# A gated Fourier-mixing block on one core: LayerNorm statistics of the first chunk shared between VectorE and ScalarE

## Chip, core and metric

The kernel runs on one core of one Trainium2 chip. The metric is the device time of one execution in microseconds (us). Engines are named as in the profile: PE is TensorE's matrix multiply, PEld its weight load, DVE is VectorE, ACT is ScalarE, SP is the engine whose queue issues most transfers.

## What is computed

The input `x` has 2048 rows (tokens) of 512 numbers. Each row is normalised, the normalised matrix is mixed by a Fourier transform along both axes (real part), and the result is multiplied by a gate that a two-layer network computes from the same normalised rows.

```python
xn = (x - mean(x)) / sqrt(var(x) + 1e-5)            # per row, 512 numbers
a, b = xn @ Wd_re.T, xn @ Wd_im.T                   # 512 x 512
s = Ws_re @ a - Ws_im @ b                           # 2048 x 2048
h = relu(xn @ w1 + b1) ** 2                         # 512 -> 1792
g = silu(h @ w2 + b2)                               # 1792 -> 512
out = x + s * g
```

## The kernel before

Every product is made in fp32r from two parts of each operand: a high part (ACT copies the fp32 source into fp32r, `split_hi`, line 134) and a low part (DVE subtracts the high part from the source, `split_lo`, line 137). A product is three matmuls: high by high, high by low, low by high (`PASSES`).

The sequence transform comes first, in eight chunks of 256 output columns each. Chunks 0 and 1 are made plainly (`products`, matmuls on line 370), chunks 2 to 7 by a seven-product scheme (`mm`, line 355). The hidden-dimension transform (line 739), the first layer (line 739) and the second layer (line 845) follow. The order in which instructions stand on each engine is the order of the code: the schedule is manual, each engine works through its own list strictly from the front, and an instruction that waits holds back all that stand behind it.

The change is in **chunk 0**, lines 458 to 518, where the normalised input is also made. Chunk 0 has eight steps, j = 0 to 7. Step j treats 256 rows of `x`, as two halves of 128 (h = 0 and 1; half 1 lies 1024 rows further on). For a half, the names are:

- `x` (code: `xr[j]`): the raw rows, 128x512, loaded by SP (`load_x`, line 199). Four buffers.
- `bn_stats` and `bn_aggr` (`ln_stats`, lines 205 and 206, DVE): mean and variance into `stats`.
- the root of the variance (`ln_root`, line 213, ACT), then `ln_rstd` (lines 219 to 223, DVE): a reciprocal and one step of refinement, four tiny instructions.
- `xn` (`ln_xn`, line 230, DVE): the normalised half.
- `xc` high and low (`xc_parts`, lines 134 and 137): the parts of `xn`, the stationary operand of PE.
- `u` (`raw`, line 266): the raw columns of the sequence matrix, 128x1024 for a step, three buffers; `g` high and low (`plain_parts`): its parts, the moving operand, two buffers in turn.

PE's work in a step is 24 matmuls of 128x512 into four banks: for h = 0 and then h = 1, three groups of four (in chunk 0 all four high by high, then all four high by low, then all four low by high). So the first group of a half needs the high parts of `xc` and `g`, the second the low part of `g`, the third the low part of `xc`.

In step 0 the loads of `x` and `u` are split by halves, and 16 matmuls on zeros (line 475; 8 in bf16, 8 in fp32r) keep PE at work until the first operands are there. SP issues the loads in the order x0 (two halves), u0 (two halves), x1, u1, x2, u2, x3; later ones follow inside the loop, each when its buffer is free. In the loop, step j on DVE is: `ln_rstd(j)`, `xn` of both halves, `g` low, `xc` low of half 0, statistics of both halves of step j + 1, `xc` low of half 1.

After chunk 0, `plain_out` (ACT, line 144) takes the four banks out, and the sums and splits of the seven-product scheme (`sums`, line 248) begin on DVE beside chunk 1.

Of the kernel before, what the change touches and what calls it, by code (L numbers as in the profile page):

```python
# [10 lines left out]
AF = mybir.ActivationFunctionType  # L11
# [3 lines left out]
S, D, F = 2048, 512, 1792  # L15
# [3 lines left out]
NC = S // CW  # L19
TC = 512  # L20
NTC = S // TC
WARM = 8, 8
PLAIN = 2

ASIDE = 4.2
# [103 lines left out]
def fnet_gated_kernel(ctx, tc, x, xt, ct, wd, w1, w2, b1, b2, out):  # L129
    nc = tc.nc  # L130
    ctx.enter_context(tc.manual_schedule(engines=None))

    def split_hi(hi, lo, src):
        nc.scalar.activation(hi, src, AF.Copy)  # L134

    def split_lo(hi, lo, src):
        nc.vector.tensor_tensor(lo, src, hi.bitcast(F32), op=ALU.subtract)  # L137
# [5 lines left out]
    def copy(to, src, scale=1.0):  # L143
        nc.scalar.activation(to, src, AF.Copy, scale=scale)
# [7 lines left out]
    eps = pool.tile([P, 1], F32, name="eps")  # L152
    stats = pool.tile([P, 2, 2, NJ], F32, name="stats")
# [10 lines left out]
    def bank(tag, name):  # L164

        return acc.tile([P, 512], F32, tag=tag, name=name)

    def buf(tag, shape, name, dtype=F32):
        return pool.tile(shape, dtype, tag=tag, bufs=3 if tag == "u" else 1, name=name)

    def operand_buf(tag, name, step, shape=(2, 7, 256)):

        first = START.get(tag, 0)
        skip = (step - first) % 4 * LANE
        size = shape[0] * shape[1] * shape[2]
        room = ROOM.get(tag, 0)
        flat = buf(tag, [P, size + (room or skip)], name, F32R)
        a, b, c = shape
        return flat[:, skip:skip + size].rearrange("p (a b c) -> p a b c", a=a, b=b, c=c)

    def bcast(src, n):
        return bass.AP(tensor=src.tensor, offset=src.offset, ap=[[0, P], [1, n]])

    def halves(ap):
        return ap.rearrange("p (a b) -> p a b", a=2)
# [5 lines left out]
    small = buf("e", [P, 3, 16], "small")  # L191

    xr, xn32 = {}, {}

    def load_x(j, hs=slice(0, 2)):

        if j not in xr:
            xr[j] = buf(f"pq{j // 2 % 2}{j % 2}", [P, 2, D], f"x{j}")
        nc.sync.dma_start(xr[j][:, hs], x.rearrange("(h j p) d -> j p h d", h=2, p=P)[j][:, hs])

    def ln_stats(j, hs=slice(0, 2)):
        t = xr[j]
        for h in range(hs.start, hs.stop):
            bn = small[:, j % 3, 6 * h:6 * h + 6]
            nc.vector.bn_stats(bn, t[:, h])
            nc.vector.bn_aggr(stats[:, :, h, j], bn)

    root = {}

    def ln_root(j, hs=slice(0, 2)):  # L210
        n = hs.stop - hs.start
        t = root[j] = small[:, j % 3, 12:16]
        nc.scalar.activation(t[:, 0:n], stats[:, 1, hs, j], AF.Sqrt, bias=eps)

    def ln_rstd(j, hs=slice(0, 2)):
        n = hs.stop - hs.start
        y, q = root[j][:, 0:n], root[j][:, 2:2 + n]
        var = rstd = stats[:, 1, hs, j]
        nc.vector.reciprocal(y, y)

        nc.vector.scalar_tensor_tensor(q, var, EPS, y, op0=ALU.add, op1=ALU.mult)
        nc.vector.scalar_tensor_tensor(q, q, -0.5, y, op0=ALU.mult, op1=ALU.mult)
        nc.vector.scalar_tensor_tensor(rstd, q, 1.5, y, op0=ALU.add, op1=ALU.mult)

    def ln_xn(j, h):
        if j % ND == 0 and h == 0:
            xn32[j, "tile"] = buf(f"wd{j // ND}", [P, ND, 2, D], f"xn32_{j}")
        if h == 0:
            xn32[j] = xn32[j // ND * ND, "tile"][:, j % ND]
        nc.vector.tensor_scalar(xn32[j][:, h], xr[j][:, h], stats[:, 0, h, j:j + 1], stats[:, 1, h, j:j + 1],  # L230
                                op0=ALU.subtract, op1=ALU.mult)

    def xc_parts(j, h):
        s = slice(2 * h, 2 * h + 2)
        return XC[j][:, s, HI, :], XC[j][:, s, LO, :], halves(xn32[j][:, h])
# [26 lines left out]
    def load_c(c, j, hs=slice(0, 2)):  # L262
        if (c, j) not in raw:
            raw[c, j] = buf("u", [P, 8, CW], f"u{c}_{j}")
        q = slice(2 * hs.start, 2 * hs.stop)
        nc.sync.dma_start(raw[c, j][:, q], ct[c, j, :, q])

    def plain_parts(c, j, hs=slice(0, 2)):
        if (c, j) not in part:
            part[c, j] = operand_buf("g" + "ab"[j % 2], f"g{c}_{j}", 0 if (c, j) == (PLAIN - 1, NJ - 1) else 3 if j in TURNED else 1, (2, 4, CW))  # L270
        g, r = part[c, j], raw[c, j]
        s = slice(2 * hs.start, 2 * hs.stop)
        return g[:, HI, s], g[:, LO, s], r[:, s]
# [87 lines left out]
    def products(c, j, h):  # L361

        for passes in [PASSES] if c else [[q] for q in PASSES]:
            for k in range(ND):
                one_product(c, j, h, k, passes)
# [8 lines left out]
    one, two = slice(0, 1), slice(1, 2)  # L374
# [91 lines left out]
    load_x(3)  # L466

    warm = bank("b30", "warm")
    idle = buf("wd1", [P, 768], "idle")
    for count, zeros in zip(WARM, (idle[:, 0:256].bitcast(mybir.dt.bfloat16), idle[:, 256:768])):  # L470
        nc.vector.memset(zeros, 0.0)
        if zeros.dtype == F32:
            zeros = zeros.bitcast(F32R)
        for _ in range(count):
            nc.tensor.matmul(warm, zeros[:, 0:P], zeros, start=True, stop=True)
    ln_stats(0)
    ln_root(0)
    split_hi(*plain_parts(0, 0, one))
    ln_rstd(0)
    for h, hs in enumerate((one, two)):  # L480
        ln_xn(0, h)
        split_hi(*xc_parts(0, h))
        if h == 0:
            split_hi(*plain_parts(0, 0, two))
    for hs in (one, two):
        split_lo(*plain_parts(0, 0, hs))
    split_lo(*xc_parts(0, 0))
    ln_stats(1)
    g = plain_parts(0, 1)
    split_hi(*g)  # L490
    ln_root(1)
    split_lo(*xc_parts(0, 1))
    for h in range(2):
        products(0, 0, h)
    load_c(0, 3)
# [1 line left out]
    for j in range(1, NJ):  # L497
        ln_rstd(j)
        for h in range(2):
            ln_xn(j, h)  # L500
            split_hi(*xc_parts(j, h))
        split_lo(*g)
        load_c(*order[j + 3])
        if j + 4 < NJ:
            load_x(j + 4)
        split_lo(*xc_parts(j, 0))
        if j + 1 < NJ:
            ln_stats(j + 1)
            ln_root(j + 1)
        split_lo(*xc_parts(j, 1))  # L510
        for h in range(2):
            products(0, j, h)
        g = plain_parts(*order[j + 1])
        split_hi(*g)
        if j == 2:
            nc.sync.dma_start(b1s, b1)
            nc.sync.dma_start(b2s, bcast(b2, D))
# [62 lines left out]
    for n, s in enumerate(steps):  # L580
        c, j = s
# [4 lines left out]
        for p in FIRST if j == 0 and c > PLAIN else ORDER:  # L586
# [5 lines left out]
            a, b = PRODUCTS[p]  # L592
# [161 lines left out]
    class YUnit(Unit):  # L754

        y = None
# [183 lines left out]
    for u in range(2, NC):  # L940
        n = 2 * u + 2
# [82 lines left out]
    for n in range(NTC * NP):  # L1024
        c, p = divmod(n, NP)
# [102 lines left out]
def _launch(arrays, out_shape):  # L1128
    import numpy as np
    import concourse.bacc as bacc  # L1130
    from concourse.bass_utils import run_bass_kernel_spmd

    nc = bacc.Bacc("TRN2", target_bir_lowering=False, num_devices=1, dynamic_dma_scratch_size=1024)
    feed, args = {}, []
    for name, v in arrays.items():
        v = np.ascontiguousarray(v)
        feed[f"in_{name}"] = v
        args.append(nc.dram_tensor(f"in_{name}", v.shape, mybir.dt.from_np(v.dtype), kind="ExternalInput").ap())
    args.append(nc.dram_tensor("out_0", out_shape, F32, kind="ExternalOutput").ap())
    with tile.TileContext(nc, schedule_with_timeline_sim=True) as tc:  # L1140
        fnet_gated_kernel(tc, *args)
    r = run_bass_kernel_spmd(nc, [feed], core_ids=[0])
    return r.results[0]["out_0"]
# [25 lines left out]
```

## Time and profile before

| what | value |
|---|---|
| median of 3 runs (lowest to highest) | 677.21 us (676.71 to 678.49) |
| the profiled execution | 678.35 us, of which the span in the trace is 676.5 us |
| busy share of the span | PE 99%, PEld 96%, DVE 89%, ACT 54%, POOL 1% |
| bytes moved | 150.82 MB, mean 223 GB/s |
| chunk 0, first real matmul to chunk 1's first | 7.64 to 53.23 us |
| chunk 1 | 53.23 to 97.29 us |

The busy share of PE counts the modelled ends of pipelined matmuls, so 99% does not mean that no matmul could start earlier. Whether PE is held up shows better in the starts of successive matmuls and in the waits of the weight loads. Times in a timeline are microseconds from the start of the span; a row gives start, busy time, engine, line, operation, output, inputs, shape and count, and in brackets how long the engine had been idle before and what ended that.

### The profile page before, as it was taken

Reading aid. Unit: us, or ns where it says so; the run is one execution under the profiler, and the core shown is the slowest. Engines: PE = TensorE matmul, PEld = TensorE weight load, DVE = VectorE, ACT = ScalarE, POOL = GpSimd, SP = SyncE. Lnnn points to the kernel's source line nnn. Section 1 sums busy time; section 2 is a strip of 40 time slices with the busy share of each in tenths; the row PEclk is TensorE's granted clock in tenths of the full one; section 3 lists DMA queues with packets and bytes.
Section 4 is the critical chain, followed back from the end, with each engine's and each line's share of the span. In section 5 each row is a group of like instructions: output and inputs, shape, how many; then the busy total and the mean of one; then the engine's idle time right before and its main releaser. Section 6 shows DMA issues by size and latency. Waiting matters only on the chain.

```text
span 676.5 us, 13148 instructions
## 1 busy us (share of the span) xinstructions
PE 668.4 (99%) x5440; PEld 646.2 (96%) x5440; DVE 602.3 (89%) x840; ACT 366.8 (54%) x487; POOL 8.8 (1%) x11
## 2 busy tenths in 40 slices
PE   9999999999999999999999999999999999999997
PEld 6778889999999999999999999999999999999996
DVE  7999978999999999799889989877878879999996
ACT  3444754544535354444464547788778855454451
POOL 0000000000000000000000000000000000101010
PEclk9999999999999999999999999999999999999999
DMA  8525678546646784759578647665755956777775
GB/s 296 207 91 215 204 268 305 200 162 199 218 163 231 241 289 155 265 179 358 178 249 285 216 187 295 219 253 199 279 174 191 347 209 214 184 226 191 217 217 140
DMA packets 51723, 150.82 MB, mean 223 GB/s; under 512 B 4944, under 2 KB 19536, under 8 KB 50256
## 3 DMA queue, kind: packets, MB, share of 16 engines
q1 hardware_dynamic: 43552, 129.28, 55.9%
q10 hardware_dynamic: 6208, 18.88, 7.1%
q0 software_dynamic: 1904, 1.84, 2.0%
q8 instruction: 42, 0.69, 0.4%
q14 instruction: 17, 0.14, 0.1%
HBM read 101.98 MB, written 47.99 MB: 222 GB/s over the span
## 4 chain that ended last, share of the span: by engine, by line
PE 88%; DVE 5%; DMA 4%; issue 1%; ACT 1%; SPq 0%; DVEq 0%
PE m L355 33%; PE m_o L845 12%; PE r_B L739 12%; PE pq_b L370 8%; PE r_A L739 7%; PE r_C L739 4%; PE m_last L845 4%; PE r_D L739 4%; DMA yraw<-pqd 2%; PE pq_ba L370 2%; PE pq_bb L370 1%; PE pq_bc L370 1%; DMA hr<-hd 1%; DMA u<-in_ct 1%; DVE yg L137 1%
## 5 line engine op out<-in xcount | busy, mean ns | idle before, releaser
L355 PEld LDWEIGHTS m<-g,xc 128*128 128x128 f32 x2016 | 228.7, 188 | 0.1
L355 PE MATMUL m<-g,xc 128*128 128x256 f32 x2016 | 228.7, 276 | 0.0
L134 ACT ACTIVATE g<-u 128x1792 fp32r<-128x1792 f32 (+2 forms) x65 | 99.0, 1523 | 124.6 <-PE m L355 95.5
L137 DVE TENSOR_TENSOR g<-u,g 128x1792 fp32r<-128x1792 f32 (+2 forms) x65 | 116.8, 1797 | 17.6 <-ACT g L134 16.8
L845 PE MATMUL m_o<-w,g 128*128 128x256 f32 x882 | 101.1, 276 | 0.3 <-DVE g L137 0.3
L845 PEld LDWEIGHTS m_o<-w,g 128*128 128x128 f32 x882 | 100.4, 188 | 0.7 <-DVE g L137 0.7
L134 ACT ACTIVATE g<-hr 128x1792 fp32r<-128x1792 f32 (+2 forms) x31 | 48.2, 1564 | 42.4 <-DVE hr L289 23.3
L370 PE MATMUL pq_b<-g,xc 128*128 128x512 f32 x240 | 66.4, 395 | 0.4 <-ACT xc L134 0.4
L739 PE MATMUL r_B<-xT,w 128*128 128x256 f32 x504 | 66.5, 276 | 0.0
L739 PEld LDWEIGHTS r_B<-xT,w 128*128 128x128 f32 x504 | 61.4, 188 | 0.0
L137 DVE TENSOR_TENSOR g<-hr,g 128x1792 fp32r<-128x1792 f32 (+2 forms) x31 | 56.7, 1838 | 2.9 <-ACT g L134 2.8
L370 PEld LDWEIGHTS pq_b<-g,xc 128*128 128x128 f32 x240 | 43.7, 188 | 13.2 <-ACT xc L134 3.0
L739 PE MATMUL r_A<-xT,w 128*128 128x256 f32 x336 | 42.8, 276 | 0.0
L739 PEld LDWEIGHTS r_A<-xT,w 128*128 128x128 f32 x336 | 40.3, 188 | 0.0
L739 PE MATMUL r_B<-wdp,yg 128*128 128x256 f32 x288 | 36.2, 277 | 1.1 <-DVE y L749 1.1
L739 PEld LDWEIGHTS r_B<-wdp,yg 128*128 128x128 f32 x288 | 34.2, 188 | 1.5 <-DVE y L749 1.3
L277 DVE TENSOR_TENSOR u<-u 128x512 f32<-128x512 f32 x48 | 32.9, 685 | 2.2 <-DMA u<-in_ct 2.2
L845 PE MATMUL m_last<-w,g 128*128 128x256 f32 x294 | 33.5, 276 | 0.0
L845 PEld LDWEIGHTS m_last<-w,g 128*128 128x128 f32 x294 | 33.4, 188 | 0.0
L134 ACT ACTIVATE yg<-yraw 128x1792 fp32r<-128x1792 f32 x13 | 22.3, 1712 | 8.9 <-DVE yraw L286 8.4
L137 DVE TENSOR_TENSOR yg<-yraw,yg 128x1792 fp32r<-128x1792 f32 x13 | 26.1, 2018 | 0.3 <-ACT yg L134 0.3
L739 PE MATMUL r_C<-xT,w 128*128 128x256 f32 x168 | 23.6, 276 | 0.0
(181 smaller groups left out, 870.6 us busy)
## 6 DMA issues: line engine op xcount, KB each, us to landing
u<-in_ct SPq DMA_DIRECT2D x63, 512.0 KB, 3.7
hd<-h ACTq DMA_DIRECT2D x28, 512.0 KB, 3.6
hr<-hd SPq DMA_DIRECT2D x28, 512.0 KB, 3.8
wdp<-wdd SPq DMA_DIRECT2D x8, 896.0 KB, 6.9
yraw<-pqd SPq DMA_DIRECT2D x13, 512.0 KB, 5.8
pqd<-c SPq DMA_DIRECT2D x6, 1024.0 KB, 6.1
w<-w1d SPq DMA_DIRECT2D x6, 896.0 KB, 9.2
y<-y ACTq DMA_DIRECT2D x8, 512.0 KB, 5.6
```

The lines of the kernel that those rows point to most:

```text
L134: nc.scalar.activation(hi, src, AF.Copy)
L137: nc.vector.tensor_tensor(lo, src, hi.bitcast(F32), op=ALU.subtract)
L277: nc.vector.tensor_tensor(t[:, 0:2], r[:, 0:1].to_broadcast([P, 2, 256]), r[:, 1:3], op=ALU.add)
L355: nc.tensor.matmul(ps[:, d], w[:, a_, d * P:(d + 1) * P], halves(mv(b_)), start=first and d == 0 and (a_, b_) == (HI, HI), stop=last and ( ...
L370: nc.tensor.matmul(accs[c][k], w, part[c, j][:, b_, 2 * h:2 * h + 2], start=j == 0 and h == 0 and (a_, b_) == (HI, HI), stop=j == NJ - 1 a ...
L739: nc.tensor.matmul(self.region(REGION[k]), w, mv, start=i == 0 and k in (1, 7), stop=i == len(ops) - 1, skip_group_check=True)
L845: nc.tensor.matmul(m[:, i * 256:(i + 1) * 256], ready[n][:, a_, H_SLOT[a], i * P:(i + 1) * P], W2[p][:, b_, b], start=p == 0 and i == 0 an ...
```

## The change

There are four edits, all in chunk 0.

1. In each step from 1 to 7, the statistics of half 1 move from DVE to ACT. `ln_stats` now treats half 0 only. `ln_mean` copies the half with scale 1/512 into a scratch bank of PSUM (`junk`), adding up along the row into the mean; `ln_var` squares (mean - x) in the same way into a sum; a third, tiny instruction multiplies that sum by 1/512. So DVE loses one `bn_stats` and one `bn_aggr` in each of seven steps, and ACT gains two passes over 128x512 and one 128x1 instruction.
2. In step 0 the chain from statistics to `xc` is made half by half: a root and an `ln_rstd` for each half, not one of both.
3. The order of step 0 on DVE and ACT is another: `g` low of half 0 now stands ahead of `xn` of half 1, `g` low of half 1 behind the statistics of step 1, and `ln_mean` of step 1 ahead of `xc` high of half 1 on ACT.
4. 14 warming matmuls, not 16 (8 in bf16, 6 in fp32r).

```diff
-WARM = 8, 8
+WARM = 8, 6
...
-    def ln_stats(j, hs=slice(0, 2)):
-        t = xr[j]
-        for h in range(hs.start, hs.stop):
-            bn = small[:, j % 3, 6 * h:6 * h + 6]
-            nc.vector.bn_stats(bn, t[:, h])
-            nc.vector.bn_aggr(stats[:, :, h, j], bn)
+    def ln_stats(j, h=0):
+        bn = small[:, j % 3, 6 * h:6 * h + 6]
+        nc.vector.bn_stats(bn, xr[j][:, h])
+        nc.vector.bn_aggr(stats[:, :, h, j], bn)
+
+    def ln_mean(j, h):
+
+        nc.scalar.activation(junk, xr[j][:, h], AF.Copy, scale=1.0 / D, accum_out=stats[:, 0, h, j:j + 1])
+
+    def ln_var(j, h):
+
+        total = small[:, j % 3, 6 * h:6 * h + 1]
+        nc.scalar.activation(junk, xr[j][:, h], AF.Square, bias=stats[:, 0, h, j:j + 1], scale=-1.0, accum_out=total)
+        copy(stats[:, 1, h, j:j + 1], total, 1.0 / D)
...
+    junk = bank("b31", "junk")
...
-    ln_stats(0)
-    ln_root(0)
+    for h, hs in enumerate((one, two)):
+        ln_stats(0, h)
+        ln_root(0, hs)
     split_hi(*plain_parts(0, 0, one))
-    ln_rstd(0)
-    for h, hs in enumerate((one, two)):
-        ln_xn(0, h)
-        split_hi(*xc_parts(0, h))
-        if h == 0:
-            split_hi(*plain_parts(0, 0, two))
-    for hs in (one, two):
-        split_lo(*plain_parts(0, 0, hs))
+    ln_rstd(0, one)
+    ln_xn(0, 0)
+    split_hi(*xc_parts(0, 0))
+    split_lo(*plain_parts(0, 0, one))
+    split_hi(*plain_parts(0, 0, two))
+    ln_rstd(0, two)
+    ln_mean(1, 1)
+    ln_xn(0, 1)
+    split_hi(*xc_parts(0, 1))
     split_lo(*xc_parts(0, 0))
     ln_stats(1)
+    ln_var(1, 1)
+    ln_root(1)
+    split_lo(*plain_parts(0, 0, two))
+    split_lo(*xc_parts(0, 1))
     g = plain_parts(0, 1)
     split_hi(*g)
-    ln_root(1)
-    split_lo(*xc_parts(0, 1))
...
             ln_stats(j + 1)
+            ln_mean(j + 1, 1)
+            ln_var(j + 1, 1)
             ln_root(j + 1)
```

The rows below are the instructions of one engine in their order. The last number of a name only tells buffers apart; `xc0` is the operand of step 0, `x1` the rows of step 1, `g0_1` the columns of chunk 0, step 1.

ACT from the first root to the operands of step 1, before:

```order
L213 ACTIVATE small_129<-stats_68,eps_67 128x2
L134 ACTIVATE g0_0_176<-u0_0_138 128x512
L134 ACTIVATE xc0_121<-xn32_0_182 128x2x256
L134 ACTIVATE g0_0_176<-u0_0_138 128x512
L134 ACTIVATE xc0_121<-xn32_0_182 128x2x256
L134 ACTIVATE g0_1_195<-u0_1_143 128x1024
L213 ACTIVATE small_129<-stats_68,eps_67 128x2
L134 ACTIVATE xc1_126<-xn32_0_182 128x2x256 x2
```

The same place of ACT with the change:

```order
L220 ACTIVATE small_129<-stats_68,eps_67 128x1 x2
L134 ACTIVATE g0_0_176<-u0_0_138 128x512
L134 ACTIVATE xc0_121<-xn32_0_182 128x2x256
L134 ACTIVATE g0_0_176<-u0_0_138 128x512
L208 ACTIVATE junk_152,stats_68<-x1_141 128x512
L134 ACTIVATE xc0_121<-xn32_0_182 128x2x256
L213 ACTIVATE junk_152,small_129<-x1_141,stats_68 128x512
L144 ACTIVATE stats_68<-small_129 128x1
L220 ACTIVATE small_129<-stats_68,eps_67 128x2
L134 ACTIVATE g0_1_202<-u0_1_143 128x1024
L134 ACTIVATE xc1_126<-xn32_0_182 128x2x256 x2
```

The mean of x1 stands ahead of the second `xc0`, the square pass and the tiny copy behind it, and the root of step 1 has moved ahead of `g0_1`.

DVE from the first `xn` of step 0 to the last `xc` low of step 0, before:

```order
L230 TENSOR_SCALAR xn32_0_182<-x0_135,stats_68 128x512 x2
L137 TENSOR_TENSOR g0_0_176<-u0_0_138,g0_0_176 128x512 x2
L137 TENSOR_TENSOR xc0_121<-xn32_0_182,xc0_121 128x2x256
L205 BN_STATS small_129<-x1_141 128x6
L206 BN_AGGR stats_68<-small_129 128x2
L205 BN_STATS small_129<-x1_141 128x6
L206 BN_AGGR stats_68<-small_129 128x2
L137 TENSOR_TENSOR xc0_121<-xn32_0_182,xc0_121 128x2x256
```

The same place of DVE with the change:

```order
L236 TENSOR_SCALAR xn32_0_182<-x0_135,stats_68 128x512
L137 TENSOR_TENSOR g0_0_176<-u0_0_138,g0_0_176 128x512
L225 RECIPROCAL small_129<-small_129 128x1
L227 SCALAR_TENSOR_TENSOR small_129<-stats_68,small_129 128x1
L228 SCALAR_TENSOR_TENSOR small_129<-small_129 128x1
L229 SCALAR_TENSOR_TENSOR stats_68<-small_129 128x1
L236 TENSOR_SCALAR xn32_0_182<-x0_135,stats_68 128x512
L137 TENSOR_TENSOR xc0_121<-xn32_0_182,xc0_121 128x2x256
L203 BN_STATS small_129<-x1_141 128x6
L204 BN_AGGR stats_68<-small_129 128x2
L137 TENSOR_TENSOR g0_0_176<-u0_0_138,g0_0_176 128x512
L137 TENSOR_TENSOR xc0_121<-xn32_0_182,xc0_121 128x2x256
```

The second `xn` now has a reciprocal chain of its own ahead of it, one pair of statistics is gone, and the second `g0_0` low stands behind the statistics of x1.

More of the change, by code (lines that the diff above doesn't have):

```diff
@@ L199, in load_x @@
         nc.sync.dma_start(xr[j][:, hs], x.rearrange("(h j p) d -> j p h d", h=2, p=P)[j][:, hs])
-    def ln_stats(j, hs=slice(0, 2)):
-        t = xr[j]
-        for h in range(hs.start, hs.stop):
-            bn = small[:, j % 3, 6 * h:6 * h + 6]
-            nc.vector.bn_stats(bn, t[:, h])
-            nc.vector.bn_aggr(stats[:, :, h, j], bn)
+    def ln_stats(j, h=0):
[8 more added lines that the diff above has]
+        copy(stats[:, 1, h, j:j + 1], total, 1.0 / D)
     root = {}
     def ln_root(j, hs=slice(0, 2)):
-        n = hs.stop - hs.start
-        t = root[j] = small[:, j % 3, 12:16]
-        nc.scalar.activation(t[:, 0:n], stats[:, 1, hs, j], AF.Sqrt, bias=eps)
+        root[j] = small[:, j % 3, 12:16].rearrange("p (a h) -> p a h", a=2)
+        nc.scalar.activation(root[j][:, 0, hs], stats[:, 1, hs, j], AF.Sqrt, bias=eps)
     def ln_rstd(j, hs=slice(0, 2)):
-        n = hs.stop - hs.start
-        y, q = root[j][:, 0:n], root[j][:, 2:2 + n]
+        y, q = root[j][:, 0, hs], root[j][:, 1, hs]
         var = rstd = stats[:, 1, hs, j]
```

## The prediction, made before the changed kernel was run

> **What bounds the kernel now.** I read the chain that ended last first, because it says which engine a saved microsecond has to reach.
>
> ```profile
> PE 88%; DVE 5%; DMA 4%; issue 1%; ACT 1%; SPq 0%; DVEq 0%
> ```
>
> PE carries the chain, so the question is whether chunk 0 lets PE run at its own speed. Its own speed shows in the chain in chunk 1, where one start follows another every 12 matmuls:
>
> ```profile
> 53.39 2.04 PE pq_b L370 x9
> ...
> 56.11 2.04 PE pq_b L370 x9
> ```
>
> 12 matmuls take 2.72 us, 24 take **5.45**. Next, PE's timeline at the starts of chunk 0, step 1, step 7 and chunk 1, and the waits of the weight loads:
>
> ```profile
> 7.64 0.73 PE L370 MATMUL pq_b<-g,xc 128*128 128x512 f32 x2
> ...
> 13.85 0.73 PE L370 MATMUL pq_b<-g,xc 128*128 128x512 f32 x2 [0.40 <-ACT xc L134]
> ...
> 47.63 0.73 PE L370 MATMUL pq_b<-g,xc 128*128 128x512 f32 x2
> ...
> 53.23 2.20 PE L370 MATMUL pq_b<-g,xc 128*128 128x512 f32 x9
> ```
>
> ```profile
> PEld pq_b L370 <- ACT xc L134: 3.0, 8, 0.8
> ```
>
> Steps 1 to 7 take 53.23 - 13.85 = 39.38 us, **5.63** each, and step 0 takes 6.21. Eight weight loads, one per step, wait for `xc`. Behind ACT's copy stands DVE, whose timeline of one step has no idle entry:
>
> ```profile
> 34.32 0.16 DVE L219 RECIPROCAL small<-small 128x2 f32<-128x2 f32 x1
> ...
> 35.10 1.00 DVE L230 TENSOR_SCALAR xn<-x,stats 128x512 f32<-128x512 f32 x2
> 36.02 1.22 DVE L137 TENSOR_TENSOR g<-u,g 128x1024 fp32r<-128x1024 f32 x1
> 37.16 0.68 DVE L137 TENSOR_TENSOR xc<-xn,xc 128x512 fp32r<-128x512 f32 x1
> 37.76 0.69 DVE L205 BATCH_NORM_STATS2 small<-x 128x6 f32<-128x512 f32 x1
> 38.48 0.18 DVE L206 BATCH_NORM_AGGREGATE stats<-small 128x2 f32<-128x6 f32 x1
> 38.58 0.66 DVE L205 BATCH_NORM_STATS2 small<-x 128x6 f32<-128x512 f32 x1
> 39.27 0.18 DVE L206 BATCH_NORM_AGGREGATE stats<-small 128x2 f32<-128x6 f32 x1
> 39.37 0.66 DVE L137 TENSOR_TENSOR xc<-xn,xc 128x512 fp32r<-128x512 f32 x1
> 39.95 0.16 DVE L219 RECIPROCAL small<-small 128x2 f32<-128x2 f32 x1
> ```
>
> Reciprocal to reciprocal is 39.95 - 34.32 = 5.63 us: DVE sets the pace of chunk 0, and PE could go only 0.18 faster per step.
>
> **The steady steps.** DVE loses the second pair of statistics: 39.37 - 38.58 = 0.79 us of each step, so its round becomes 4.84, well under PE's 5.45. PE then sets the pace. The new work lies on ACT, in this gap:
>
> ```profile
> 35.68 1.15 ACT L134 ACTIVATE xc<-xn 128x512 fp32r<-128x512 f32 x2 [0.57 <-DVE xn L230]
> 39.49 0.30 ACT L213 ACTIVATE small<-stats,eps 128x2 f32<-128x2 f32 x1 [2.66 <-DVE stats L206]
> ```
>
> ACT idles 2.66 us between the second `xc` and the root. No row shows an accumulating pass. The nearest are plain copies of 128x512 (0.63, below) and, for what a row sum may add at the end, ACT's smallest instruction:
>
> ```profile
> 2.03 0.20 ACT L458 ACTIVATE stats<-eps 128x1 f32<-128x1 f32 x1
> ```
>
> The mean is 0.63. The square pass has a bias read from memory; the root with such a bias takes 0.30, this one 0.20, so I add 0.10: 0.73. The tiny copy is 0.20. For the row sum I bound the extra by 0 (it is written beside the pass; nothing in the rows lets it gain) and 0.30 (a separate instruction as dear as the root), and take **0.20** a pass as the value of the nearest row, hence e = 0.40 for both.
>
> The round through ACT, from reciprocal to reciprocal: 2.51 until both `xc` are out (34.32 to 36.83), 0.63, 0.73, 0.20 and 0.30, and four hand-overs of about 0.03: 4.5, with e 4.9. That is still under 5.45. What the 0.79 buys is thus PE's own shortfall, not 0.79.
>
> Step 1 keeps its first group's exposed weight load (5.60 instead of 5.45), since it starts late; steps 2 to 7 go at 5.45. Chunk 1 starts 5.60 + 6 x 5.45 = **38.3** after step 1, 1.08 sooner than the 39.38 of before.
>
> **The start.** One root per half frees the first half earlier:
>
> ```profile
> 4.18 0.18 DVE L206 BATCH_NORM_AGGREGATE stats<-small 128x2 f32<-128x6 f32 x1
> ...
> 4.98 0.18 DVE L206 BATCH_NORM_AGGREGATE stats<-small 128x2 f32<-128x6 f32 x1
> 5.59 0.17 DVE L219 RECIPROCAL small<-small 128x2 f32<-128x2 f32 x1 [0.43 <-ACT small L213]
> ...
> 6.38 1.00 DVE L230 TENSOR_SCALAR xn<-x,stats 128x512 f32<-128x512 f32 x2
> ...
> 8.75 0.69 DVE L137 TENSOR_TENSOR xc<-xn,xc 128x512 fp32r<-128x512 f32 x1
> 9.36 0.69 DVE L205 BATCH_NORM_STATS2 small<-x 128x6 f32<-128x512 f32 x1
> ...
> 11.79 0.17 DVE L219 RECIPROCAL small<-small 128x2 f32<-128x2 f32 x1 [0.16 <-ACT small L213]
> ```
>
> ```profile
> 5.26 0.30 ACT L213 ACTIVATE small<-stats,eps 128x2 f32<-128x2 f32 x1 [3.03 <-DVE stats L206]
> 5.73 0.63 ACT L134 ACTIVATE g<-u 128x512 fp32r<-128x512 f32 x1 [0.17 <-DMA u<-in_ct]
> 6.96 0.63 ACT L134 ACTIVATE xc<-xn 128x512 fp32r<-128x512 f32 x1 [0.60 <-DVE xn L230]
> ...
> 13.16 1.16 ACT L134 ACTIVATE xc<-xn 128x512 fp32r<-128x512 f32 x2 [1.40 <-DVE xn L230]
> ```
>
> The first root can run at 4.46, right after 4.18 + 0.18, so the reciprocal goes at 5.08, when DVE is through with the second half, and not at 5.59. The first `xc` and the first real matmul come 0.51 earlier, at 7.13. Half 0's twelve matmuls last about 2.9 us, to 10.05.
>
> Now the moved ACT pass. The mean of x1 stands ahead of the second `xc` on ACT, and needs x1:
>
> ```profile
> 2.60 0.43 SPq L199 DMA_DIRECT2D x<-in_x  x1
> ```
>
> ```profile
> x<-in_x SPq DMA_DIRECT2D x1, 512.0 KB, 6.6
> ```
>
> The load of x1 is issued at 2.60 and lands 6.6 later, at **9.2**. In before only the `bn_stats` at 9.36 needed it, which DVE reached later anyway. In the changed kernel ACT would be free at 7.6, waits to 9.25 and copies to 9.88; the second `xc`, whose `xn` is ready at 8.4, runs 9.78 to 10.41 (these passes overlap by 0.1). So PE stalls from 10.05 to about 10.45. Then the square pass (10.31 to 11.04), the tiny copy (to 11.27), the root (to 11.60), the reciprocal at 11.64 (11.79 before), `xn` 0.79 later for 0.54, `xc`, and step 1's first matmul 0.69 after that `xc` starts (as 13.16 to 13.85): 13.70. With e = 0.40 on this path it is **14.10**, against 13.85: the 0.51 won is lost again.
>
> The first `g` low of half 1 stands behind x1's statistics (about 10.1 to 10.7), which is early enough for its group at 11.5; SP issues u3 and x4 behind it, two microseconds later than before, but they are used two steps on. The two warming matmuls cost nothing if the first real ones follow at full speed:
>
> ```profile
> 1.22 6.39 PE L475 MATMUL warm<-idle 128*128 128x512 bf16 x16 [1.22 <-DVE idle L471]
> ```
>
> ```profile
> L475 PEld LDWEIGHTS warm<-idle x8: 188/330/337, 4.2 to 7.0; 128*128 128x128 f32 x8
> ```
>
> The loads of the warming matmuls fall from 330 to 188 ns within the sixteen, so PE speeds up before 7.0, and fourteen (16 less two of about 0.23) still reach 7.1. If it sped up later, matmuls of half 0 would be slow by 0.2 each, and up to two of them vanish in PE's stall at 10.05.
>
> The Trainium skill ("TensorE: Matmul & The Clock Gate", section "Part 1: The HAM clock gate") speaks against removing them: the clock opens after one free-running window of 3.4 us full of work, at a phase that differs from run to run. By that rule some executions would run the first real matmuls at half rate. The trace agrees as to a fall in mid-warming, and shows one phase only; by the rule the sum would move by a few tenths at most.
>
> **The sum.** Chunk 1 starts at 14.10 + 38.3 = 52.4 instead of 53.23, **0.83 earlier**. Does the rest follow? DVE will have worked ahead, but not keep that lead:
>
> ```profile
> 54.67 1.08 ACT L134 ACTIVATE g<-u 128x1024 fp32r<-128x1024 f32 x1
> ```
>
> ```profile
> 55.79 1.23 DVE L137 TENSOR_TENSOR g<-u,g 128x1024 fp32r<-128x1024 f32 x1
> ```
>
> ```profile
> 69.89 1.68 PEld L370 LDWEIGHTS pq_b<-g,xc 128*128 128x128 f32 x8 [0.36 <-DVE g L137]
> ```
>
> This `g` high on ACT stands behind the copies out of chunk 0's banks, which wait for PE, and DVE's low part at 55.79 waits for it. So DVE is tied to PE again there, chunk 1's one late weight load of 0.36 and its like stay, and all that follows moves by the same 0.83. Of the profiled execution (678.35, a span of 676.5 and 1.85 around it) 677.5 remains; from the median, which is 1.14 lower, 677.21 - 0.83 = **676.4 us**, a gain of 0.12%. With e from 0 to 0.60 and x1 0.3 earlier or later, step 1 starts at 13.4 to 14.6 and the gain is 0.3 to 1.5: the forecast's own range is 675.7 to 676.9.
>
> **The rivals.** *ACT becomes the bound (slower).* If an accumulating pass takes twice a copy and a read besides, e = 2 x (0.63 + 0.20) = 1.66: step 1 starts at 15.36, the round through ACT is 6.1 and replaces 5.45 in six steps: 15.36 + 6 x 6.1 + 5.6 = 57.6, **4.4 later: 681.6**. From e = 1.0, 0.5 a pass, the round through ACT passes PE's, and by 1.05 the gain is gone. Against it: 128x512 copies at 0.63 show ACT at full rate in every form that it runs here. For it: no row shows the form.
>
> The Trainium skill ("ScalarE: Activation LUTs", section "Rules for kernel authors") says that plain adds and multiplies belong on VectorE, which is faster per element; that is the direction of this rival. The rows here do not bear it out as far as they go, since DVE has no idle time and ACT 2.66 a step.
>
> *The wait for x1 does not bite (faster).* If x1 landed by 8.4, or if half 0 hid it, ACT's chain to step 1 would start 0.8 sooner, step 1 at 13.3 (12.9 with e = 0); with chunk 1's late loads gone too (0.36 and about as much) the gain is 1.6 to 2.3: **675.2**. For it: the landing is a single figure in a crowded queue. Against it: the loads ahead of x1 and behind it are the same as before.
>
> *The gain is swallowed later (no change).* If some later transfer is what paces the part between chunk 7 and the hidden transform, where the chain leaves PE, the 0.83 vanishes: **677.2**. Against it: every transfer there starts from a result of PE's.
>
> **How the numbers follow.** I give the forecast 0.54, the swallowed gain 0.10, the faster rival 0.22, the slower one 0.14. A measurement of this kernel tells about 0.3%, 2.0 us, from no change: below 675.2 is faster, above 679.2 slower. Some six tenths of the faster rival (0.13) and a little of what lies below the forecast's own range (0.05) are below, the slower rival above: faster 0.18, same 0.68, slower 0.14. The range reaches to the middle of the faster rival and over the swallowed gain with the scatter of the runs before: 674.9 to 677.9.
>
> **What would show it.** Right: DVE idle in every step of chunk 0, PE 5.45 from step to step, step 1 starting near 14.1 and chunk 1 near 52.4; on ACT the first mean starting at 9.2 with x1 as its releaser, and PE idle before half 1 of step 0. Wrong: steps of over 5.6 with weight loads waiting for `xc` (ACT's round), passes on ACT of over 1.1 us, step 1 starting before 13.4, or chunk 1 starting earlier without the end doing so.

## The result and the profile after

| | before | after |
|---|---|---|
| median | 677.31 us (17 runs) | **675.57 us** (17 runs) |
| profiled execution, span | 678.35, 676.5 us | 674.92, 673.1 us |

The ratio is 0.9968, 95% interval 0.9957 to 0.9979: 1.74 us or 0.32% faster by the medians. The forecast was 676.4, a gain of 0.83; the time lies inside the range of 674.9 to 677.9, a little below the forecast's own range of 675.7 to 676.9. The gain is about twice the forecast's. Some executions of several kernels here, before and after alike, are 3 to 5 us longer than the rest, with the second layer's matmuls at 281 instead of 276 ns in the four traces of such executions; medians of later runs contain some of them, so the traces of chunk 0 decide below.

The profiled executions differ by more than the medians, 3.43 us, and chunk 0 has only part of that. PE's timeline of the changed kernel at the first real matmul, step 1, step 2, step 7 and chunk 1:

```profile
7.18 0.71 PE L376 MATMUL pq_b<-g,xc 128*128 128x512 f32 x2
...
12.83 0.73 PE L376 MATMUL pq_b<-g,xc 128*128 128x512 f32 x2
...
18.42 0.62 PE L376 MATMUL pq_b<-g,xc 128*128 128x512 f32 x2
...
45.64 0.62 PE L376 MATMUL pq_b<-g,xc 128*128 128x512 f32 x2
...
51.08 2.20 PE L376 MATMUL pq_b<-g,xc 128*128 128x512 f32 x9
```

Step 1 starts 1.02 earlier (12.83 for 13.85), and from there to chunk 1 it takes 38.25 instead of 39.38: another 1.13. Chunk 1 starts 2.15 earlier. The 0.62 of a step's first pair, 0.73 before, shows that its weight load no longer waits. The waits of the weight loads, up to the end of chunk 1:

```profile
PEld pq_b L376 <- DVE g L137: 0.8, 3, 0.4
PEld pq_b L376 <- ACT xc L134: 0.8, 2, 0.5
```

Two waits for `xc` are left of eight. On ACT, the same stretch at the start of the changed kernel:

```profile
5.44 0.61 ACT L134 ACTIVATE g<-u 128x512 fp32r<-128x512 f32 x1
6.45 0.63 ACT L134 ACTIVATE xc<-xn 128x512 fp32r<-128x512 f32 x1 [0.40 <-DVE xn L236]
6.99 0.61 ACT L134 ACTIVATE g<-u 128x512 fp32r<-128x512 f32 x1
8.10 0.60 ACT L208 ACTIVATE junk<-x 128x512 f32<-128x512 f32 x1 [0.50 <-DMA x<-in_x]
8.64 0.19 ACT L208 ACTIVATION_READ_ACCUMULATOR junk<-x 128x1 f32 x1
8.73 0.61 ACT L134 ACTIVATE xc<-xn 128x512 fp32r<-128x512 f32 x1
9.25 0.67 ACT L213 ACTIVATE junk<-x,stats 128x512 f32<-128x512 f32 x1
9.87 0.19 ACT L213 ACTIVATION_READ_ACCUMULATOR junk<-x,stats 128x1 f32 x1
10.09 0.20 ACT L144 ACTIVATE stats<-small 128x1 f32<-128x1 f32 x1
10.32 0.30 ACT L220 ACTIVATE small<-stats,eps 128x2 f32<-128x2 f32 x1
```

The mean waits for x1, as forecast, but x1 is there at 8.1 and not at 9.2:

```profile
x<-in_x SPq DMA_DIRECT2D x1, 512.0 KB, 5.5
```

So the root of step 1 is done at 10.62, and it is no longer what comes last. DVE's rows from the first `g` low to the reciprocal of step 1, and the reciprocals of two later steps:

```profile
6.33 0.68 DVE L137 TENSOR_TENSOR g<-u,g 128x512 fp32r<-128x512 f32 x1
...
10.18 0.68 DVE L137 TENSOR_TENSOR xc<-xn,xc 128x512 fp32r<-128x512 f32 x1
10.78 0.16 DVE L225 RECIPROCAL small<-small 128x2 f32<-128x2 f32 x1
...
34.98 0.16 DVE L225 RECIPROCAL small<-small 128x2 f32<-128x2 f32 x1
39.82 0.16 DVE L225 RECIPROCAL small<-small 128x2 f32<-128x2 f32 x1
```

No row of this stretch has an idle time: the reciprocal goes at 10.78 because DVE has then worked through its own list of step 0, 4.45 us after the first `g` low, and step 1's first matmul follows 2.05 later. In the later steps DVE's round is 39.82 - 34.98 = 4.84, as forecast, but DVE does not idle in each step. It runs ahead of PE, and its first idle time is 3.00 us at 46.94, where it waits for ACT's `g` high of chunk 1.

The remaining 1.3 us of the difference between the two profiled executions lies far behind chunk 0. In the hidden transform of before, PE waited once, and DVE there for a transfer:

```profile
PE r_B L739 <- DVE y L749: 1.1, 1, 1.1
```

```profile
DVE yraw L283 <- DMA yraw<-pqd: 2.2, 2, 1.9
```

In the changed kernel DVE's wait at that place is smaller and PE's is gone:

```profile
DVE yraw L289 <- DMA yraw<-pqd: 1.4, 2, 0.8
```

Whether that belongs to the change is a question for the repeats.

### The profile page after: what moved, and what is told of

It reads as the page before. It is cut to its first block, busy times and chain, and to the rows that moved or that the text cites. A ratio compares the mean times of both kernels' runs of the same rounds, so it can differ in the third digit from the quotient of the medians.

```text
span 673.1 us, 13176 instructions
## 1 busy us (share of the span) xinstructions
PE 666.6 (99%) x5438; PEld 646.9 (96%) x5438; DVE 597.4 (89%) x830; ACT 378.3 (56%) x523; POOL 8.8 (1%) x11
## 4 chain that ended last, share of the span: by engine, by line
PE 95%; DVE 2%; DMA 2%; issue 0%; ACT 0%; DVEq 0%
PE m L361 34%; PE r_B L752 13%; PE m_o L858 12%; PE r_A L752 9%; PE pq_b L376 8%; PE r_C L752 4%; PE r_D L752 4%; PE m_last L858 4%; PE pq_ba L376 2%; PE pq_bc L376 2%; PE pq_bb L376 2%; DMA hr<-hd 1%; PE warm L482 1%; DVE g L137 0%; DMA out<-z 0%
## 5 line engine op out<-in xcount | busy, mean ns | idle before, releaser
L752 PE MATMUL r_D<-xT,w 128*128 128x256 f32 x168 | 23.6, 276 | 0.0
```

The lines of the kernel that those rows point to most:

```text
L752: nc.tensor.matmul(self.region(REGION[k]), w, mv, start=i == 0 and k in (1, 7), stop=i == len(ops) - 1, skip_group_check=True)
```

## The experiments

**Theory A:** the steady steps gain 1.1 us because DVE no longer paces them; step 0 gains what the landings of the first loads allow, which differ from execution to execution. **Rival B:** the changed kernel itself brings the early landing and the early step 1. **Rival C:** ACT sets or shares the pace, or the two parts are not separate.

In what follows, "u0" is the start of ACT's first `g` (it waits for u0's first half where that lands late, and else follows the root), "g low" the start of DVE's first `g` low, and "x1" the landing of that load. Runs for which no median is given are one execution each, of which only the trace is used.

### Both kernels again

No edit. Before:

> The kernel before once more. Theory A: x1 lands anywhere from 8.0 to 9.3 us here too, and it changes nothing, because step 1 waits for the DVE; step 1 near 13.85, chunk 1 near 53.2. Rival B: x1 at 9.2 within 0.2. The wait of 1.1 us of PE in the hidden transform: if it is scatter it can be missing or of another size; if it belongs to the kernel it is 1.1 again.

The changed kernel, twice:

> The changed kernel once more, to see what of its trace returns. Theory A (the landing of x1 scatters from execution to execution): x1 lands anywhere from 8.0 to 9.3 us, and step 1 starts at 12.83, or at the landing plus 4.6 us where that is later. Rival B (the changed kernel itself makes x1 land at 8.1): 8.1 again within 0.2, step 1 at 12.8. Both: chunk 1 starts 38.25 us after step 1, and the time is about 675.6 us.

> The changed kernel again, on the same chip as the run before. The landing of u0's first half plus 1.2 us gives the first real matmul (not under 7.1); step 1 is at the later of the first g low on DVE plus 6.5 us and the landing of x1 plus 4.6; chunk 1 38.3 us behind it.

The medians of the two repeats of the changed kernel were 675.78 and 676.3 us (ratios 0.9974, interval 0.9953 to 0.9996, and 0.9989, 0.9967 to 1.001; 12 executions each). In the second of them DVE and PE started as in the first trace. In the first, u0 landed late, and these are its rows of ACT and of DVE:

```profile
6.72 0.63 ACT L134 ACTIVATE g<-u 128x512 fp32r<-128x512 f32 x1 [1.20 <-DMA u<-in_ct]
7.26 0.61 ACT L134 ACTIVATE xc<-xn 128x512 fp32r<-128x512 f32 x1
```

```profile
7.39 0.69 DVE L137 TENSOR_TENSOR g<-u,g 128x512 fp32r<-128x512 f32 x1 [0.98 <-ACT g L134]
```

The first `g` stands ahead of the first `xc` on ACT and waits for u0 until 6.72; `xc`, ready to go at 6.45 in the first trace, goes at 7.26. On DVE the first `g` low now stands ahead of the second half's `ln_rstd` and `xn`, so all of that waits too. What the one chain per half had won is lost behind a load, and step 1 started at 13.89, no earlier than before. The five traces of the two kernels (us; the last column is from step 1 to chunk 1):

| kernel | u0 | g low | x1 | first matmul | step 1 | to chunk 1 |
|---|---|---|---|---|---|---|
| before, first trace | 5.73 | | 9.2 | 7.64 | 13.85 | 39.38 |
| before, repeat | 5.59 | | 7.6 | 7.69 | 13.64 | 39.37 |
| changed, first trace | 5.44 | 6.33 | 8.1 | 7.18 | 12.83 | 38.25 |
| changed, repeat 1 | 6.72 | 7.39 | 8.7 | 7.93 | 13.89 | 38.28 |
| changed, repeat 2 | 5.51 | 6.40 | 8.0 | 7.20 | 12.90 | 38.27 |

x1 lands at 9.2 and 7.6 in two executions of the kernel before, and between 8.0 and 8.7 in three of the changed one, so an early landing does not need the change and rival B falls. Before, x1 did not set step 1. The 0.21 between its two starts of step 1 comes from u1, in the first trace:

```profile
10.51 1.06 ACT L134 ACTIVATE g<-u 128x1024 fp32r<-128x1024 f32 x1 [1.88 <-DMA u<-in_ct]
11.47 0.28 ACT L213 ACTIVATE small<-stats,eps 128x2 f32<-128x2 f32 x1
```

The root of step 1 stood behind the `g` of u1, which went at 10.51 (8.94 in the repeat), so the root went at 11.47 (11.13). The change moves that root ahead of the `g` and takes this wait away as well; the prediction compared with 13.85, which contains it.

The wait in the hidden transform does not belong to the change either: before's repeat has no such PE wait, and the kernel with step 0 alone, below, has one of 0.6 us. From chunk 1 to the first matmul of the second layer it took 481.8 us in before's first trace, 480.5 in its repeat, and 480.4, 480.7 and 480.9 in the changed kernel's three.

### One part alone: the steady steps, or step 0

The loop as changed, step 0 as before (16 warming matmuls, the old order, step 1's statistics on DVE); the main lines:

```diff
-WARM = 8, 6
+WARM = 8, 8
...
+    ln_stats(0)
+    ln_stats(0, 1)
+    ln_root(0)
...
     ln_stats(1)
-    ln_var(1, 1)
-    ln_root(1)
...
+    ln_stats(1, 1)
```

> Only the part in the loop: statistics of half 1 on ACT for steps 2 to 7; step 0, step 1's statistics and the 16 warming matmuls as before. If the pieces of the gain are separate (start and step 0; pace of the steps), step 1 starts at 13.85, the steps after it go at 5.45 us, chunk 1 starts at about 52.2, and the time is 1.0 to 1.1 us below before (676.2). Rival (the pace comes with the early start, since step 1 leaves the DVE a lead): steps stay over 5.55 us and chunk 1 starts at 52.8 or later, a gain under 0.5 us.

Step 1 started at 13.68, chunk 1 38.29 later at 51.97. The median was 676.99 (0.9996, interval 0.9971 to 1.0021), which decides nothing; the trace does. The pace of 5.45 comes without any early start. That part's share of the whole time is not shown by itself.

Step 0 as changed, the loop as before:

```diff
-            ln_mean(j + 1, 1)
-            ln_var(j + 1, 1)
+            ln_stats(j + 1, 1)
```

> Only the part in step 0: one chain per half, the new order, the mean and variance of step 1's half 1 on ACT, 14 warming matmuls; in the loop the DVE makes the statistics of both halves as before. If the pieces are separate, the first real matmul is at 7.18, step 1 at 12.83 (with x1 landing by 8.2), the steps at 5.63, chunk 1 at about 52.2, and the time 1.0 us below before (676.2). Rival (step 0's gain is given back in the steps): step 1 early, but chunk 1 at 53.0 or later and no gain.

The steps went at 5.63 again (39.38 to chunk 1), but step 1 started at 13.77, not at 12.83: u0 was there at 6.32, x1 at 9.1. The median was 676.96 (0.9994, 0.9973 to 1.0015). So the run shows that step 0 alone does not change the pace, but this execution does not show what step 0 can gain. The rows of ACT are those that the prediction had foreseen for a late x1:

```profile
7.37 0.61 ACT L134 ACTIVATE g<-u 128x512 fp32r<-128x512 f32 x1
9.16 0.60 ACT L208 ACTIVATE junk<-x 128x512 f32<-128x512 f32 x1 [1.17 <-DMA x<-in_x]
9.70 0.19 ACT L208 ACTIVATION_READ_ACCUMULATOR junk<-x 128x1 f32 x1
9.79 0.61 ACT L134 ACTIVATE xc<-xn 128x512 fp32r<-128x512 f32 x1
```

ACT stands 1.17 us in front of the mean, with the second `xc` behind it. 9.16 + 4.6 = 13.76 is step 1.

### The landing of x1, moved on purpose

```diff
-        load_x(j)
         load_c(0, j)
+        load_x(j)
```

> The changed kernel, with the loads of x1 and x2 issued behind those of u1 and u2, so that x1 lands later. Theory A (step 1 starts at the landing of x1 plus 4.6 us, through the mean that stands ahead of the second xc on ACT, or 6.5 us after the first g low on DVE where that is later): x1 lands at 9.0 to 10.5, and step 1 starts at that plus 4.6, 13.6 to 15.1, with PE idle before half 1 of step 0. Rival B (ACT's wait hides behind the twelve matmuls of half 0): step 1 stays within 0.3 us of what the first g low gives. Both: 38.3 us from step 1 to chunk 1.

The mean, which waits for x1, went at 9.25 and step 1 started at 13.85. That is the landing plus 4.6, where the first `g` low (6.60) would have given 13.1. Half 1 of step 0 started at 10.54. The wait does not hide.

The same, with the mean behind the second `xc`:

```diff
-    ln_mean(1, 1)
     ln_xn(0, 1)
     split_hi(*xc_parts(0, 1))
+    ln_mean(1, 1)
```

> As the run before, but the mean of step 1's half 1 stands behind the second xc of step 0 on ACT. Theory A: half 1 of step 0 no longer waits for x1; the chain from x1 loses one pass of 0.5 us, so step 1 starts at the landing plus 4.1 us, or 6.5 us after the first g low. Rival B: no difference beyond 0.1 us in either.

x1 landed at 9.43, half 1 started at 10.12, and step 1 at 13.65: the landing plus 4.2, 0.1 more than I had expected, since the row sum that the `xc` used to cover is now in the open (the square pass starts 0.22 after it). By one execution of each, the order on ACT is worth 0.4 us when x1 is late.

### Statistics of step 1 left on DVE

```diff
-    ln_mean(1, 1)
...
-    ln_var(1, 1)
+    ln_stats(1, 1)
```

> The changed kernel, but the statistics of step 1's half 1 stay on DVE (0.79 us more in step 0's list), and ACT has no pass for them. Step 1 then starts 7.3 us after the first g low on DVE (6.5 plus 0.79), 13.6 to 14.6, whatever x1 does, and it starts later than before's 13.6 to 13.85 where u0 lands late: the new order of step 0 without the pass on ACT gains nothing. 38.3 us from step 1 to chunk 1.

The first `g` low started at 6.55 and step 1 at 13.85, 7.30 later. x0 came 0.22 later here than in the changed kernel's first trace (DVE's first statistics at 3.64, not 3.42); without that step 1 would be at 13.63, where before's repeat has 13.64. The early chain alone gives nothing; taking 0.79 off DVE in step 0 is what brings step 1 forward.

### How much room ACT has

One, then three more passes of 128x512 in each step (n is 1, then 3), their result unused:

```diff
             ln_var(j + 1, 1)
+            for _ in range(n):
+                nc.scalar.activation(junk, xr[j + 1][:, 1], AF.Copy)
             ln_root(j + 1)
```

> The changed kernel with one more copy of 128x512 to the scratch bank on ACT in each of the steps 2 to 7's statistics (work that has no use). Theory A (PE sets the pace of the steps; ACT's round is 4.56 us from its own rows, of PE's 5.45): the round becomes 5.1 and from step 1 to chunk 1 it stays at 38.3 us. Rival C (ACT already sets the pace or shares in it): 0.5 us more in each of six steps, 41 us.

> The same with three more copies. Theory A: the round through ACT is 4.56 + 3 x 0.53 = 6.15 and passes PE's 5.45, so that from step 1 to chunk 1 it takes 6 x 6.15 + 5.6 = 42.5 us instead of 38.3, and weight loads wait for xc in every step. If ACT can run further ahead than its round suggests, it stays below 40.

With one pass it stays at 38.28 us, and ACT goes from root to root in 4.96. With three it is 42.97 (42.5 expected). ACT and DVE with three, from one root to the next reciprocal:

```profile
29.08 0.28 ACT L220 ACTIVATE small<-stats,eps 128x2 f32<-128x2 f32 x1
29.27 1.04 ACT L134 ACTIVATE g<-u 128x1024 fp32r<-128x1024 f32 x1
30.76 1.16 ACT L134 ACTIVATE xc<-xn 128x512 fp32r<-128x512 f32 x2 [0.46 <-DVE xn L236]
31.82 0.58 ACT L208 ACTIVATE junk<-x 128x512 f32<-128x512 f32 x1
...
32.56 0.69 ACT L213 ACTIVATE junk<-x,stats 128x512 f32<-128x512 f32 x1
...
33.52 1.85 ACT L523 ACTIVATE junk<-x 128x512 f32<-128x512 f32 x3
35.31 0.28 ACT L220 ACTIVATE small<-stats,eps 128x2 f32<-128x2 f32 x1
```

```profile
35.62 0.17 DVE L225 RECIPROCAL small<-small 128x2 f32<-128x2 f32 x1 [1.31 <-ACT small L220]
```

Root to root is 6.23 us, DVE waits 1.31 for ACT, and 6 x 6.23 + 5.6 = 43.0. Rival C falls for the changed kernel: its ACT round has room for one pass more and not for three. Without them the round is about 4.5 by either run (4.96 or 6.23, less about 0.5 to 0.6 for each added pass).

### The warming matmuls

```diff
-WARM = 8, 6
+WARM = 8, 8
```

> The changed kernel with 16 warming matmuls. Where the operands are there by 7.1, the first real matmul comes at 7.4 to 7.5, behind the last warming one, and step 1 by at most that much later; where u0 lands late, no difference. Rival (two fewer leave PE slow at the start): the changed kernel's first group of four takes longer than 1.1 us, and here it takes 0.9 to 1.05.

u0 came at 6.13, and the sixteen had ended 0.24 us before the first real matmul at 7.33, so this run cannot show what two fewer are worth. Step 1 was at 13.30, again `g low` (6.79) plus 6.5. In the changed kernel's own runs PE was fast when the first real matmul came: the first group of four took 1.01 to 1.05 us, also after an idle time of 2.1, and step 1's takes as long (1.04). The fourteen warming ones took 6.15 us in its first trace, 4.59 in its second and 5.62 in its third, so the point at which PE speeds up does move, as the Trainium skill ("TensorE: Matmul & The Clock Gate", section "Part 1: The HAM clock gate") says of its free-running window. An execution in which it came too late was not met.

### An attempt to do better

u0 issued from ACT's queue beside SP's loads of x0 (`load_c` now takes the queue), and the mean behind the second `xc`:

```diff
+    for hs in (one, two):
+        load_c(0, 0, hs, nc.scalar)
     nc.scalar.activation(stats[:, 1, 0, 0:1], eps, AF.Sqrt)
     for hs in (one, two):
         load_x(0, hs)
-    for hs in (one, two):
-        load_c(0, 0, hs)
...
-    ln_mean(1, 1)
     ln_xn(0, 1)
     split_hi(*xc_parts(0, 1))
+    ln_mean(1, 1)
```

> The changed kernel with two things more: the two loads of u0 are issued from ACT's queue at the start, beside SP's loads of x0 (so SP reaches x1 0.9 us sooner), and the mean of step 1's half 1 stands behind the second xc of step 0. Theory A (what scatters in the changed kernel is the landing of u0's first half, which both the first g on ACT and through it the DVE wait for, and the landing of x1): u0 lands by 4.5, x1 by 8.3, so that the first real matmul is at 7.1 to 7.5 (later than 7.2 only if x0 shares its transfer time with u0), step 1 at 12.7 to 13.1 and chunk 1 at 51.0 to 51.4, and the time is 0.3 to 0.6 us under the changed kernel's. Rival (x0 is held up as much as u0 gains): first matmul at 7.8 or later and no gain.

The rival came true. DVE's first statistics, in this kernel and then in the changed kernel's run on the same chip:

```profile
4.61 0.69 DVE L203 BATCH_NORM_STATS2 small<-x 128x6 f32<-128x512 f32 x1 [2.90 <-DMA x<-in_x]
```

```profile
3.49 0.69 DVE L203 BATCH_NORM_STATS2 small<-x 128x6 f32<-128x512 f32 x1 [1.78 <-DMA x<-in_x]
```

x0 lands 1.1 us later, the first matmul moves to 8.51, step 1 to 14.41, and the median is 677.31 us, 0.9981 of before (0.9964 to 0.9998), against 676.3 for the changed kernel beside it. The first `g` low (7.71) plus 6.5 would give 14.2: with the mean behind the second `xc` it is ACT's chain that ends last, by 0.2, so that order costs something where x1 is not late. The Trainium skill ("Trainium Kernel Development and Optimization", section "Key Constraints") says that all queues share the same 16 transfer engines and that a second queue only saves time of issue; the run agrees.

## Why the prediction was right, point by point

- **DVE paces chunk 0 and PE takes over: right.** 38.3 us from step 1 to chunk 1 was forecast. Ten traces with the loop as changed and at most one added pass gave 38.25 to 38.30; three with the old loop gave 39.37 or 39.38. This is 1.1 of the gain, and the traces with one part alone show it by itself. DVE's round came out at the 4.84 forecast. Of the signs listed, the steps of 5.45 came, but not "DVE idle in every step": DVE uses its spare time to run ahead, and waits only where chunk 1's operands begin.
- **ACT's gap covers the passes: right.** The extra e was put at 0.40 a step and the round at 4.9; about 4.5 was found. A row sum costs an instruction of 0.19, close to the 0.20 taken, and the room found (one pass more, not three) brackets the limit. ACT needs more time for this work than DVE did: from the mean to the end of the tiny copy 1.78 us (13.21 to 14.99), for 0.79 on DVE. It pays all the same, because ACT had the time to spare.
- **The mean of x1 holds the second `xc`: the mechanism is real, but it did not set step 1.** This is the step that failed. "Lands 6.6 later, at 9.2" was taken from one execution as if it were the kernel's, with 0.3 to either side. Where its place in the queue is unchanged, x1 lands anywhere from 7.4 to 9.2 in the runs here. With 9.16 and 9.25 step 1 came at 13.77 and 13.85, below the 14.10 forecast (4.6 after the landing instead of 4.9). In the three traces of the changed kernel x1 landed at 8.0 to 8.7, and step 1 came at 12.83, 12.90 and 13.89, later than x1 plus 4.6 in each.
- **A path that the prediction left out: DVE's own list of step 0.** It followed step 1 only through ACT. The list takes 6.5 from the first `g` low to step 1, and where x1 is early, this ends last. What starts it is x0 (first and third trace) or u0 (second). The prediction quoted the first `g` waiting for u0 at 5.73 and treated that as fixed; it starts between 5.35 and 6.72 in the runs that load as before, and the changed order puts more behind it. What the runs show in place of 14.10: step 1 starts at the later of `g` low plus 6.5 and x1's landing plus 4.6. That holds within 0.1 us for the three traces of the changed kernel and for step 0 alone, the late x1, the one and three extra passes (`g` low 6.46 and 6.24, step 1 12.96 and 12.75) and 16 warming matmuls. The two constants were read from earlier traces; the third trace, the late x1 and step 1's statistics on DVE (6.5 plus 0.79) were forecast with them.
- **The first matmul at 7.13: right when u0 is early** (7.18, 7.20), else u0 plus 1.2 (7.93 in repeat 1).
- **All that follows moves along: right.** Chunk 1's late weight loads stay (0.35 and 0.29 in the changed kernel, 0.36 and 0.29 before), and behind chunk 1 the traces scatter by as much for one kernel as between the kernels. Of the 3.43 between the profiled executions, 2.15 come from chunk 0 and 1.3 from a wait for a transfer that before's repeat does not have.
- **The rivals.** "The wait for x1 does not bite" describes the three traces of the changed kernel better than the forecast does, since x1 set step 1 in none of them, though in one a late u0 cost as much. The measured 1.74 lies in its 1.6 to 2.3, beyond the forecast's own 0.3 to 1.5; but it counted chunk 1's late loads as gone, and they stay. "The gain is swallowed later" falls: the interval of the result lies wholly below 1, and the earlier start of chunk 1 accounts for the gain (below). The slower rival's mechanism is real, but begins at more than one added pass.

So the sum was right in its pace term and 0.9 too small in its start term: step 1 starts at 13.21 in the mean of the changed kernel's three traces, not at 14.10. Two of the three lie below 13.4, which the prediction had named as a sign that it is wrong, and in the first PE does not stall before half 1 of step 0 (10.05, right behind half 0). From the means of the traces, step 1 starts 0.54 earlier than before (13.75) and the steps gain 1.11: chunk 1 is 1.65 earlier, near the 1.74 of the medians. The time fell into the stated range because that range was wide, and not because the sum came out. What the two missing warming matmuls do alone stays open.

## What to carry to other kernels

Where DVE shows no idle entry and ACT has a gap in each step, moving a piece across gains, but only as much as the next engine's own pace allows, here 0.16 of the 0.79 us per step. A landing time from one profile is a sample, not a property: where an in-order engine is made to wait for a load, look at what stands behind the wait and price it for a spread of landings, from several executions. And a passage that ends in `max(this, that)` should be forecast with both arms.

## What the runs showed of the hardware

- ACT's row sum is an instruction of its own, 128x1, 0.19 us, and the next independent pass starts about 0.1 after its start: 8.64 and 8.73 above.
- Copies of 128x512 on ACT from SBUF into the scratch bank of PSUM took 0.58 to 0.60 us, those from SBUF to SBUF 0.61 to 0.63. The first write fp32 and the others fp32r, so the runs do not show which of the two makes the difference.
- Loads of 256 and 512 KB that are in flight together land with a scatter of over 1 us from execution to execution, at the same times of issue: x1, issued at 2.6, took 4.8 to 6.6 us.
